# A head's second scores, one stretch of products sooner in the first two batches

## The chip, the cores and the metric

The kernel runs on one core of a Trainium2 chip. What counts is the device time of one execution in microseconds (us). TensorE (PE in the profile) multiplies matrices, VectorE (DVE), ScalarE (ACT) and GpSimd (POOL) work on tiles, SyncE (SP) issues transfers. Each has its own queue of instructions.

## The reference

An attention layer over 4 batches of 12 heads, 448 tokens and 64 numbers to a head, and behind it two layers of the feed-forward kind over all 1792 tokens:

```python
q_n, k_n = (rmsnorm(q, g_q), rmsnorm(k, g_k))
scores = scale * np.matmul(q_n, k_n.transpose(0, 1, 3, 2))
scores = scores - np.max(scores, axis=-1, keepdims=True)
attn = np.exp(scores)
attn = attn / (np.sum(attn, axis=-1, keepdims=True) + 1e-09)
x = np.matmul(attn, v)                      # then (1792, 768)
h = x @ w_in;  r = np.maximum(h, 0.0);  x = (r * r) @ w_out
a = x @ w1;  b = x @ w2;  out = ((a * b) @ w3) @ w_out2
```

The last two products have no function between them, so the kernel multiplies their weights (`w3` and the second `w_out`) once, ahead of the layers.

## The kernel before, in words

The 48 heads run one after the other in the loop `for h in range(NH + 1)`; H is 12, the heads of a batch. The attention of a batch leaves TensorE much time, and into that time the kernel puts dense products, which a generator hands out: in heads 0 to 12 those of `w3` with `w_out2` (384 products of 384 columns, tile `mm`), from head 13 on the feed-forward layers of the batch before (1008 products of 448 columns for a batch). Each call `fill(n)` hands out one stretch of them. A head has six stretches: about five products each up to head 12, and 12 or 15 each in heads 13 to 23 (the second batch, in which a pace is set layer by layer). After head 23 the same loop goes on with the third and fourth batch, and it ends with the layers of the last batch alone.

Every product is done in three passes, because a number is held as a high and a low half: `hl` is the tile of weights with both halves. The weights of the first round come from the inputs as 64-bit words. SP loads them (`raw<-w_in`, `raw<-w_out`, `raw<-w`), ScalarE and GpSimd work on the two words (L201, L207), VectorE joins them (L214), ScalarE copies the high half (`hl<-raw`, L113) and GpSimd or VectorE subtracts the low half (`hl<-raw,hl`, L121). SP also stores the joined weights for later batches. There are four buffers of 64-bit weights, six of joined ones and four of `hl`.

The parts of a head:

- `stage_k(h + 1)`: four transposes of the next head's keys (tile `kv`, L517) and a copy by ScalarE (`kt`).
- `stage_qk(h, s)`: the scores of half s, four products (L533, L534) into two buffers `sc` in PSUM, the only two there are. VectorE takes the maxima (`nb<-sc`, L535, twice) and scales them (`nb<-nb,rr`, L536).
- `stage_exp(h, s)`: ScalarE's two exponentials of the half (`p<-sc,nb,rr`, L552). Each frees one buffer `sc`. From head 12 on, SP then copies the half with a DMA (`pw<-p`, L558).
- `stage_t(h - 1, kc)`: four transposes each of the head before (tile `pt`, L579). They read both halves of `p` or `pw`. ScalarE copies the high half (`ptr`, `pte`), and `stage_lo` has VectorE subtract the low half.
- `stage_v(h - 1)`: seven products with the values (tile `kv`, L631).

So a head's first scores and its second scores take turns in the same two buffers, and both must wait until ScalarE has done the exponentials of the half before. Tile's scheduler orders each engine's queue by what it expects to be ready. Mostly it keeps the order of the code, but it may move an instruction past its neighbours. On the chip each queue then runs in that order.

Of the kernel before, what the change touches and what calls it, by code (L numbers as in the profile page):

```python
# [30 lines left out]
def attention_moe_kernel(  # L31
# [16 lines left out]
    B, P, H, C, D = q_nat.shape  # L48
# [62 lines left out]
    def copy_on(eng, out, in_):  # L111
        if eng == "a":
            nc.scalar.activation(out=out, in_=in_, func=AF.Copy)  # L113
        elif eng == "g":
            nc.gpsimd.tensor_scalar(out=out, in0=in_, scalar1=1.0, scalar2=1.0, op0=ALU.mult, op1=ALU.mult)
        else:
            nc.vector.tensor_copy(out=out, in_=in_)
# [280 lines left out]
    def load_group(g):  # L398
        if not (0 <= g < NH // GH):
            return  # L400
        b, h0 = divmod(g * GH, H)
        qn = t1.tile([P, GH, C, D], F32, name="qn", tag="qn")
        kn = t2.tile([P, GH, C, D], F32, name="kn", tag="kn")
        if g == 0:
            nc.sync.dma_start(out=kn[:, 0:1], in_=k_nat[0, :, 0:1])
            load_head(0)
            nc.sync.dma_start(out=qn[:, 0:1], in_=q_nat[0, :, 0:1])
            load_to(0)
            nc.sync.dma_start(out=kn[:, 1:], in_=k_nat[0, :, 1:GH])
            nc.sync.dma_start(out=qn[:, 1:], in_=q_nat[0, :, 1:GH])  # L410
            load_to(1)
        else:
            nc.sync.dma_start(out=kn, in_=k_nat[b, :, h0:h0 + GH])
            nc.sync.dma_start(out=qn, in_=q_nat[b, :, h0:h0 + GH])
        grp[g] = [qn, kn, None, None]

    def load_head(h):
        if not (0 <= h < NH):
            return
        b, hh = divmod(h, H)  # L420
        t = t2.tile([128, S], F32, name="qt", tag="qt")
        nc.sync.dma_start(out=t, in_=q_t[b, hh])
        qts[h] = t

    def load_v(h):
        if not (0 <= h < NH):
            return
        b, hh = divmod(h, H)
        t = t2.tile([128, C, D], F32, name="v", tag="v")
        nc.sync.dma_start(out=t, in_=v_in[b, hh])  # L430
        vs[h] = t
# [78 lines left out]
    def stage_k(h):  # L510
        if not (0 <= h < NH):
            return
        d = heads[h]
        khl = d.pop("khl")
        ps = ps_kv.tile([128, 512], F32R, name="kv", tag="kv")
        for c in range(C):
            nc.tensor.transpose(ps[:, c * P:(c + 1) * P], khl[:, c, :], ident_r)  # L517
        kt = t2.tile([128, S], F32R, name="kt", tag="kt")
        copy_on("a", kt, ps[:, :S].bitcast(F32))
        d["kt"] = kt  # L520

    def stage_qk(h, s):
        if not (0 <= h < NH):
            return
        d = heads[h]
        nb = d["nb"] = small.tile([P, 2], F32, name="nb", tag="nb")
        c0 = 2 * s
        o = d["sc"] = [None, None]
        for j in range(2):
            c = c0 + j  # L530
            ps = ps_sc.tile([128, 512], F32, name="sc", tag="sc")
            o[j] = ps[:P, :S]
            nc.tensor.matmul(o[j], d["qh"][:, c * P:(c + 1) * P], d["kt"], start=True, stop=False)  # L533
            nc.tensor.matmul(o[j], d["ql"][:, c * P:(c + 1) * P], d["kt"], start=False, stop=True)  # L534
            nc.vector.tensor_reduce(out=nb[:, j:j + 1], in_=o[j], axis=AX.X, op=ALU.max, negate=True)  # L535
        nc.vector.tensor_tensor(out=nb, in0=nb, in1=d["rq"][:, c0:c0 + 2], op=ALU.mult)  # L536

    def stage_exp(h, s):
        if not (0 <= h < NH):
            return  # L540
        d = heads[h]
        nb, o = d.pop("nb"), d.pop("sc")
        i = h % 2
        if s == 0 and i == 0:
            sums2[h // 2] = small.tile([P, 2, C], F32, name="sm", tag="sm")
        sm = sums2[h // 2]
        c0 = 2 * s
        pp = t3.tile([P, 2, S], F32, name="p", tag="p")
        for j in range(2):
            c = c0 + j  # L550
            p = d["p"][c] = pp[:, j, :]
            nc.scalar.activation(  # L552
                out=p, in_=o[j], func=AF.Exp, scale=d["rq"][:, c:c + 1], bias=nb[:, j:j + 1],
                accum_out=sm[:, i, c:c + 1],
            )
        if h >= H:
            words = t3.tile([P, 2, S], F32R, name="pw", tag="pw")
            nc.sync.dma_start(out=words.bitcast(F32), in_=pp)  # L558
            d["p"][c0:c0 + 2] = [words[:, 0, :], words[:, 1, :]]
        if s == 1 and i == 1:  # L560
            nc.vector.tensor_scalar(out=sm, in0=sm, scalar1=1e-9, scalar2=None, op0=ALU.add)
            rs = small.tile([P, 2, C], F32, name="rs", tag="rs")
            nc.vector.reciprocal(out=rs, in_=sm)
            wide = t1.tile([P, C, 2, D], F32, name="rsw", tag="rsw")
            nc.gpsimd.tensor_scalar(
                out=wide, in0=rs.rearrange("p i c -> p c i").unsqueeze(3).to_broadcast([P, C, 2, D]),
                scalar1=1.0, scalar2=1.0, op0=ALU.mult, op1=ALU.mult,
            )
            sums2[h // 2] = wide.rearrange("p c i d -> p c (i d)")
# [21 lines left out]
    def stage_lo(h):  # L591
        if not (0 <= h < NH):
            return
        d = heads[h]
        for lo, p, hi in d["lo"]:
            sub_on("v", lo, p, hi)
        d["lo"] = []
# [25 lines left out]
    def stage_v(h):  # L623
        if not (0 <= h < NH):
            return
        d = heads.pop(h)
        vt = d["v"].rearrange("p c a d -> p c (a d)")
        ps = ps_kv.tile([128, 512], F32, name="kv", tag="kv")
        ops = [(vt[:, kc, :], m) for kc in range(4) for m in d["pt"][kc]]
        for n, (w, m) in enumerate(ops):  # L630
            nc.tensor.matmul(ps[:, :S], w, m, start=(n == 0), stop=(n == len(ops) - 1))  # L631
        i = h % 2
        r0, r1 = i * D, (1 - i) * D
        if i == 0:
            xf[0] = t2.tile([128, S], F32, name="xf", tag="xf")
        x = xf[0]
        tmp = t1.tile([128, S], F32, name="vt", tag="vt")
        copy_on("a", tmp[r0:r0 + D, :], ps[r1:r1 + D, :S])
        nc.vector.tensor_tensor(out=x[r0:r0 + D, :], in0=ps[r0:r0 + D, :S], in1=tmp[r0:r0 + D, :], op=ALU.add)

    def stage_x(h):
        if 0 <= h < NH and h % 2:
            x = xf[0]
            b, hh = divmod(h, H)
            nc.vector.tensor_tensor(out=x, in0=norms_to_rows(h), in1=x, op=ALU.mult)
            t = xp.tile([128, 2, S], F32R, name="x", tag="x")
            copy_on("a", t[:, 0, :], x)
            sub_on("g", t[:, 1, :], x, t[:, 0, :].bitcast(F32))
            xs[b, hh // 2] = t
# [4 lines left out]
    def start_fill(gen, total):  # L654
        state.update(gen=gen, credit=0.0, left=total)

    def fill(n):
        state["credit"] += n
        while state["gen"] is not None and state["credit"] > 0:
            try:  # L660
                k = next(state["gen"])
                state["credit"] -= k
                state["left"] -= k
            except StopIteration:
                state["gen"] = None
# [22 lines left out]
    for h in range(NH + 1):  # L688
        n = W3O / ((H + 1) * 6) if h <= H else MOE / (H * 6)
        load_head(h + 3)  # L690
        load_v(h + 1)
        if h % GH == 0:
            load_group(h // GH + 1)
        stage_qk(h, 0)
        fill(n)
        stage_exp(h, 0)
        if h % H != 1:
            stage_x(h - 2)
        stage_t(h - 1, 0)
        stage_t(h - 1, 1)  # L700
        fill(n)
        stage_lo(h - 1)
        if h < NH:
            v_prep(h)
        fill(n)
        stage_k(h + 1)
        stage_t(h - 1, 2)
        stage_t(h - 1, 3)
        fill(n)
        stage_lo(h - 1)  # L710
        stage_qk(h, 1)
        fill(n)
        stage_exp(h, 1)
        fill(n)
        stage_v(h - 1)
        if h % GH == 1:
            group_prep(h // GH + 1)
        head_prep(h + 2)
        if h and h % H == 0:
            fill(1e9)  # L720
            stage_x(h - 1)
            start_fill(gen_moe(h // H - 1), MOE)
# [57 lines left out]
```

## Time and profile before

| | |
|---|---|
| median of 3 runs | 1230.52 us (1227.25 to 1230.81) |
| the profiled execution | 1229.23 us |
| its span, first to last instruction | 1227.4 us |
| TensorE busy | 1173.1 us, 96% |
| VectorE, ScalarE, GpSimd busy | 689.3, 732.9, 780.1 us |
| moved by DMA | 207.63 MB, mean 169 GB/s |

The span lies 1.8 us under the time of its own execution. Busy time is time in which the engine worked on an instruction, whatever kept it from working faster. What TensorE does not work adds up to 54.3 us.

### The profile page before, as it was taken

Reading aid. Unit: us, or ns where it says so; the run is one execution under the profiler, and the core shown is the slowest. Engines: PE = TensorE matmul, PEld = TensorE weight load, DVE = VectorE, ACT = ScalarE, POOL = GpSimd, SP = SyncE. Lnnn points to the kernel's source line nnn. Section 1 sums busy time; section 2 is a strip of 40 time slices with the busy share of each in tenths; the row PEclk is TensorE's granted clock in tenths of the full one; section 3 lists DMA queues with packets and bytes.
Section 4 is the critical chain, followed back from the end, with each engine's and each line's share of the span. In section 5 each row is a group of like instructions: output and inputs, shape, how many; then the busy total and the mean of one; then the engine's idle time right before and its main releaser. Section 6 shows DMA issues by size and latency. Waiting matters only on the chain.

```text
span 1227.4 us, 19009 instructions
## 1 busy us (share of the span) xinstructions
PE 1173.1 (96%) x6258; PEld 1054.9 (86%) x6258; DVE 689.3 (56%) x1231; ACT 732.9 (60%) x1581; POOL 780.1 (64%) x772
## 2 busy tenths in 40 slices
PE   7799999998989999999999999999999999999998
PEld 4588888886878889998998999999999999999998
DVE  5699878858977773556575554745655421012100
ACT  5799877767657564666646556656545544442442
POOL 6775535655666664766776664756766556678673
PEclk9699999999999999999999999999999999999999
DMA  7775447888788865545535455444543443333342
GB/s 230 228 252 163 148 143 231 276 280 268 253 264 260 252 193 167 147 132 149 161 113 169 133 174 159 145 128 136 156 121 114 139 138 116 111 111 103 103 129 72
DMA packets 111346, 207.63 MB, mean 169 GB/s; under 512 B 12208, under 2 KB 66704, under 8 KB 111248
## 3 DMA queue, kind: packets, MB, share of 16 engines
q1 hardware_dynamic: 107792, 200.92, 53.5%
q10 hardware_dynamic: 3456, 5.51, 1.2%
q8 instruction: 49, 0.80, 0.3%
q14 instruction: 49, 0.40, 0.1%
HBM read 149.95 MB, written 27.53 MB: 145 GB/s over the span
## 4 chain that ended last, share of the span: by engine, by line
PE 60%; DMA 4%; DVE 3%; POOL 2%; ACT 1%; issue 1%; SPq 0%; DVEq 0%; POOLq 0%; ACTq 0%
PE mm L269 17%; PE mm L271 17%; PE mm L270 17%; PE kv L631 3%; PE pt L579 2%; DMA raw<-w 2%; DMA pw<-p 2%; PE sc L534 1%; PE sc L533 1%; POOL hl L121 1%; DMA kn<-k_nat 1%; PE kv L517 1%; DVE raw L214 0%; POOL x L121 0%; PE mm L620 0%
## 5 line engine op out<-in xcount | busy, mean ns | idle before, releaser
L121 POOL TENSOR_TENSOR hl<-raw,hl 128x384 fp32r<-128x384 f32 (+1 forms) x383 | 446.5, 1169 | 259.6 <-ACT hl L113 253.5
L113 ACT ACTIVATE hl<-raw 128x384 fp32r<-128x384 f32 (+1 forms) x416 | 233.8, 564 | 147.7 <-PE mm L271 84.5
L270 PE MATMUL mm<-x,hl 128*128 128x448 f32 (+1 forms) x832 | 305.8, 368 | 7.6 <-POOL x L121 7.6
L269 PE MATMUL mm<-x,hl 128*128 128x448 f32 (+1 forms) x832 | 309.4, 372 | 1.6 <-DVE gf L342 1.0
L271 PE MATMUL mm<-x,hl 128*128 128x448 f32 (+1 forms) x832 | 305.0, 367 | 3.0 <-DVE hl L121 1.8
L270 PE MATMUL mm<-act,hl 128*128 128x448 f32 (+1 forms) x640 | 235.8, 368 | 4.3 <-POOL act L121 4.3
L269 PE MATMUL mm<-act,hl 128*128 128x448 f32 (+1 forms) x640 | 237.6, 371 | 0.0
L271 PE MATMUL mm<-act,hl 128*128 128x448 f32 (+1 forms) x640 | 234.4, 366 | 0.7 <-DVE hl L121 0.7
L552 ACT ACTIVATE p<-sc,nb,rr 112x448 f32<-112x448 f32 x192 | 137.3, 719 | 73.1 <-DVE nb L536 72.3
L270 PEld LDWEIGHTS mm<-x,hl 128*128 128x128 f32 x832 | 157.5, 189 | 21.5 <-POOL x L121 9.3
L271 PEld LDWEIGHTS mm<-x,hl 128*128 128x128 f32 x832 | 157.3, 189 | 17.9 <-POOL hl L121 3.1
L269 PEld LDWEIGHTS mm<-x,hl 128*128 128x128 f32 x832 | 157.3, 189 | 15.3 <-DVE gf L342 1.4
L270 PEld LDWEIGHTS mm<-act,hl 128*128 128x128 f32 x640 | 121.6, 190 | 16.2 <-POOL act L121 6.9
L535 DVE TENSOR_REDUCE nb<-sc 112x1 f32<-112x448 f32 x192 | 113.5, 617 | 36.8 <-PE sc L534 35.2
L271 PEld LDWEIGHTS mm<-act,hl 128*128 128x128 f32 x640 | 121.7, 190 | 10.6 <-DVE hl L121 1.1
L269 PEld LDWEIGHTS mm<-act,hl 128*128 128x128 f32 x640 | 121.6, 190 | 9.6
L121 DVE TENSOR_TENSOR ptr<-pt,ptr 128x448 fp32r<-128x448 f32 x144 | 86.8, 619 | 73.1 <-ACT ptr L113 72.6
L207 POOL TENSOR_SCALAR raw<-raw 128x384 uint32<-128x384 uint16 (+1 forms) x110 | 78.7, 716 | 66.1 <-DMA raw<-w_in 21.4
L214 DVE SCALAR_TENSOR_TENSOR raw<-raw 128x384 uint32<-128x384 uint32 (+1 forms) x120 | 80.9, 679 | 43.5 <-POOL hl L121 26.6
L121 POOL TENSOR_TENSOR act<-gf,act 128x448 fp32r<-128x448 f32 x80 | 97.8, 1223 | 8.9 <-DVE gf L342 3.7
L201 ACT ACTIVATE raw<-raw 128x384 f32<-128x384 f32 (+1 forms) x120 | 70.6, 598 | 52.6 <-DMA raw<-w_out 16.8
L342 DVE TENSOR_TENSOR gf<-mm,r 128x448 f32<-128x448 f32 x64 | 39.8, 622 | 94.7 <-ACT r L338 89.4
(87 smaller groups left out, 1595.2 us busy)
## 6 DMA issues: line engine op xcount, KB each, us to landing
pw<-p SPq DMA_DIRECT2D x72, 392.0 KB, 4.4
raw<-f_in SPq DMA_DIRECT2D x96, 192.0 KB, 2.4
raw<-f_out SPq DMA_DIRECT2D x72, 256.0 KB, 2.7
raw<-f SPq DMA_DIRECT2D x96, 192.0 KB, 2.3
raw<-w_in SPq DMA_DIRECT2D x32, 384.0 KB, 4.6
raw<-w_out SPq DMA_DIRECT2D x24, 512.0 KB, 5.9
raw<-w SPq DMA_DIRECT2D x32, 384.0 KB, 5.0
raw<-w3o SPq DMA_DIRECT2D x48, 256.0 KB, 2.7
```

What stands on the lines that cost most here:

```text
L113: nc.scalar.activation(out=out, in_=in_, func=AF.Copy)
L121: e.tensor_tensor(out=out, in0=in0, in1=in1, op=ALU.subtract)
L201: nc.scalar.activation(out=hi, in_=hi, func=AF.Prelu, scale=2.0**-112, alpha=-(2.0**32))
L207: nc.gpsimd.tensor_scalar(out=t[:, :n, 0], in0=low, scalar1=2.0**-13, scalar2=2.0**-14 - 0.5, op0=ALU.mult, op1=ALU.add)
L214: nc.vector.scalar_tensor_tensor(out=f[:, :n].bitcast(U32), in0=t[:, :n, 1], scalar=3, in1=t[:, :n, 0], op0=ALU.logical_shift_left, op1=AL ...
L269: nc.tensor.matmul(ps, w[:, 0, wk, :], x[0], start=(i == 0), stop=False)
L270: nc.tensor.matmul(ps, w[:, 0, wk, :], x[1], start=False, stop=False)
L271: nc.tensor.matmul(ps, w[:, 1, wk, :], x[0], start=False, stop=(i == last))
L342: nc.vector.tensor_tensor(out=gf, in0=ps, in1=r, op=ALU.mult)
L535: nc.vector.tensor_reduce(out=nb[:, j:j + 1], in_=o[j], axis=AX.X, op=ALU.max, negate=True)
L552: nc.scalar.activation(out=p, in_=o[j], func=AF.Exp, scale=d["rq"][:, c:c + 1], bias=nb[:, j:j + 1], accum_out=sm[:, i, c:c + 1],)
L631: nc.tensor.matmul(ps[:, :S], w, m, start=(n == 0), stop=(n == len(ops) - 1))
```

## The change

In heads 0 to 23 `stage_qk(h, 1)` is called ahead of `stage_k(h + 1)` and of the third and fourth group of transposes, and so one stretch of products sooner. The call of `fill` that stood behind it goes behind `stage_exp(h, 1)`. The number of stretches in a head stays six. Heads 24 to 47 keep their order.

```diff
         fill(n)
+        even = h < 2 * H
+        if even:
+            stage_qk(h, 1)
         stage_k(h + 1)
         stage_t(h - 1, 2)
         stage_t(h - 1, 3)
         fill(n)
         stage_lo(h - 1)
-        stage_qk(h, 1)
-        fill(n)
+        if not even:
+            stage_qk(h, 1)
+            fill(n)
         stage_exp(h, 1)
         fill(n)
+        if even:
+            fill(n)
         stage_v(h - 1)
```

On TensorE's queue in the second batch the four score products leave the place behind a stretch and stand ahead of the key transposes. This is where head 17's second scores come to stand:

```order
 L270 MATMUL mm<-x,hl 128x448
 L271 MATMUL mm<-x,hl 128x448
+L533 MATMUL sc<-kt,qh 112x448
+L534 MATMUL sc<-kt,ql 112x448
+L533 MATMUL sc<-kt,qh 112x448
+L534 MATMUL sc<-kt,ql 112x448
 L517 MATMUL kv<-ident_r,khl 128x112 x4
 L579 MATMUL pt<-ident_r,pw 128x112 x4
```

They move up past four key transposes, eight `pt` transposes and the 12 products (15 in other heads) of one stretch. So 36 to 45 products now lie between the second scores and the next head's first scores, where 24 to 33 lay before.

On ScalarE's queue the exponentials move too. The place is head 16's second half, before:

```order
L113 ACTIVATE kt<-kv 128x448
L113 ACTIVATE ptr<-pt 128x448
L113 ACTIVATE pte<-pt 64x448
L201 ACTIVATE raw_3474<-raw_3474 128x384
L113 ACTIVATE acc<-mm 128x448
L113 ACTIVATE hl<-raw 128x384
L201 ACTIVATE raw_3535<-raw_3535 128x384
L113 ACTIVATE hl<-raw 128x384
L201 ACTIVATE raw_3582<-raw_3582 128x384
L552 ACTIVATE p,sm<-sc,nb,rr 112x448 x2
```

and the same place now:

```order
L113 ACTIVATE kt<-kv 128x448
L113 ACTIVATE ptr<-pt 128x448
L113 ACTIVATE pte<-pt 64x448
L552 ACTIVATE p,sm<-sc,nb,rr 112x448 x2
L113 ACTIVATE acc<-mm 128x448
L113 ACTIVATE hl<-raw 128x384
L201 ACTIVATE raw_3474<-raw_3474 128x384
L201 ACTIVATE raw_3535<-raw_3535 128x384
L113 ACTIVATE hl<-raw 128x384
L201 ACTIVATE raw_3582<-raw_3582 128x384
```

The two exponentials of the second half pass six instructions, among them two copies of high halves of weights (`hl<-raw`) and three first steps on 64-bit words (`raw<-raw`), which now stand behind them.

In the first batch the scheduler keeps less of the code's order. This is head 10's second scores now, on TensorE's queue, where before they stood behind the transposes and six more products:

```order
L270 MATMUL mm<-act,hl 128x384
L271 MATMUL mm<-act,hl 128x384
L533 MATMUL sc<-kt,qh 112x448
L534 MATMUL sc<-kt,ql 112x448
L533 MATMUL sc<-kt,qh 112x448
L534 MATMUL sc<-kt,ql 112x448
L517 MATMUL kv<-ident_r,khl 128x112 x4
L579 MATMUL pt<-ident,p 128x112 x4
L269 MATMUL mm<-act,hl 128x384
L270 MATMUL mm<-act,hl 128x384
L579 MATMUL pt<-ident,p 64x112 x4
```

## Rows read from the trace of the kernel before

**Rows 1.** Busy time of each engine in four stretches of the span.

```profile
core 0: us, PE busy (x) PEld busy (x) DVE busy (x) ACT busy (x) POOL busy (x), PEclk, DMA share, GB/s
0.00:75.00 75.00, 56.65 (x259) 41.72 (x259) 51.89 (x94) 53.40 (x114) 53.90 (x64) 0.84 0.74 229
75.00:178.00 103.00, 96.29 (x591) 86.05 (x592) 88.44 (x174) 86.53 (x194) 53.65 (x68) 1.00 0.54 170
178.00:453.00 275.00, 250.63 (x1323) 221.34 (x1324) 221.78 (x394) 183.58 (x404) 168.74 (x182) 0.98 0.80 252
453.00:1227.00 774.00, 769.49 (x4088) 705.78 (x4087) 327.14 (x571) 409.40 (x872) 503.86 (x459) 1.00 0.45 134
```

**Rows 2.** TensorE's waits, 75 to 178 us: total us, times, longest us.

```profile
PE sc L533 <- ACT p L552: 5.5, 5, 1.8
```

**Rows 3.** TensorE's waits, 178 to 453 us.

```profile
PE sc L533 <- ACT p L552: 10.2, 10, 2.4
PE pt L579 <- DMA pw<-p: 7.3, 7, 1.8
PE mm L271 <- DVE hl L121: 2.6, 2, 1.8
```

**Rows 4.** TensorE in order of time, heads 16 to 17.

```profile
272.24 0.37 PE L533 MATMUL sc<-kt,qh 128*112 128x448 f32 x1
...
278.41 1.38 PE L631 MATMUL kv<-ptr,vhl 128*128 128x448 f32 x6
...
281.36 0.46 PE L533 MATMUL sc<-kt,qh 128*112 128x448 f32 x1 [1.38 <-ACT p L552]
...
297.22 0.37 PE L533 MATMUL sc<-kt,qh 128*112 128x448 f32 x1
```

**Rows 5.** VectorE in order of time, same heads.

```profile
278.08 0.56 DVE L214 SCALAR_TENSOR_TENSOR raw<-raw 128x384 uint32<-128x384 uint32 x1 [1.51 <-POOL hl L121]
278.56 1.15 DVE L535 TENSOR_REDUCE nb<-sc 112x1 f32<-112x448 f32 x2
...
279.98 0.48 DVE L536 TENSOR_TENSOR nb<-nb,rr 112x2 f32<-112x2 f32 x1
```

**Rows 6.** ScalarE in order of time, same heads.

```profile
280.50 0.72 ACT L552 ACTIVATE p<-sc,nb,rr 112x448 f32<-112x448 f32 x1 [0.56 <-DVE nb L536]
...
290.78 0.73 ACT L552 ACTIVATE p<-sc,nb,rr 112x448 f32<-112x448 f32 x1 [0.68 <-DVE nb L536]
```

**Rows 7.** TensorE in order of time, heads 10 to 11.

```profile
154.05 0.46 PE L533 MATMUL sc<-kt,qh 128*112 128x448 f32 x1 [1.25 <-ACT p L552]
...
157.68 0.46 PE L517 MATMUL kv<-ident_r,khl 112*128 112x112 f32 x4
...
159.84 0.36 PE L533 MATMUL sc<-kt,qh 128*112 128x448 f32 x1
...
164.15 0.46 PE L533 MATMUL sc<-kt,qh 128*112 128x448 f32 x1 [0.32 <-ACT p L552]
```

**Rows 8.** ScalarE in order of time, heads 10 to 11.

```profile
157.96 0.70 ACT L552 ACTIVATE p<-sc,nb,rr 112x448 f32<-112x448 f32 x1
...
163.28 0.72 ACT L552 ACTIVATE p<-sc,nb,rr 112x448 f32<-112x448 f32 x1 [0.79 <-DVE nb L536]
```

**Rows 9.** Two of three stretches of 3.4 us at the half clock.

```profile
305.70:309.10 3.40, 3.40 (x11) 2.91 (x10) 3.40 (x6) 3.40 (x9) 1.82 (x2) 0.51 0.49 170
...
411.60:415.00 3.40, 3.40 (x11) 3.01 (x10) 2.48 (x6) 1.77 (x4) 2.85 (x4) 0.50 0.95 270
```

**Rows 10.** ScalarE's waits, 178 to 453 us.

```profile
ACT p L552 <- DVE nb L536: 23.8, 14, 4.9
```

**Rows 11.** DMA issues of the page: KB each, median us to landing.

```profile
pw<-p SPq DMA_DIRECT2D x72, 392.0 KB, 4.4
```

**Rows 12.** The chain of waits, 178 to 440 us, a piece of it.

```profile
406.25 3.63 DMA raw<-w
...
411.82 5.64 DMA raw<-w
```

## The prediction

> **What bounds the kernel now.** I read the busy times by stretch first. From 453 us on TensorE works 769.5 of 774 us, and nothing but its own work sets the time there. What it loses lies ahead of that: 18 us up to 75 us, 6.7 us from 75 to 178 us and 24.4 us from 178 to 453 us [rows 1]. The last two stretches are the heads that the change touches, apart from the first three. A microsecond that TensorE stops losing there should arrive at the end whole, since behind 453 us nobody but TensorE is waited for.
>
> TensorE's list of waits says what it lost them to. From 75 to 178 us it is nearly all one wait, first or second scores for ScalarE's exponentials: 5.5 us in 5 times [rows 2]. From 178 to 453 us the same wait takes 10.2 us in 10 times, and 7.3 us in 7 times go to transposes that wait for the DMA of `pw` [rows 3].
>
> The order of time shows which scores wait. Head 16's second scores start at 272.24 us, head 17's first ones at 281.36 us after a wait of 1.38 us, and head 17's second scores start at 297.22 us without one [rows 4]. In between, VectorE takes the maxima of head 16's second half only at 278.56 us, 6.3 us after the scores began, because a join of weights stood in front that had waited 1.51 us for GpSimd [rows 5]. ScalarE then waits 0.56 us for `nb`, and its exponential at 280.50 us frees the first buffer at 281.22 [rows 6]. TensorE starts 0.14 us behind that. On the other side, head 17's first exponential frees its buffer at 290.78 + 0.73 = 291.51 us [rows 6], 5.7 us before the second scores want it. So one side waits and the other has room.
>
> **The change part by part.** No instruction is added or removed. What moves is the second scores, with the maxima, the exponentials and (second batch) the DMA of `pw` that follow from them.
>
> How far: between 272.24 and 278.41 us lie 4 scores and 24 products, so one such matmul takes 6.17 / 28 = 0.22 us [rows 4]. A stretch of 12 is 2.6 us. Four key transposes, eight `pt` transposes and six products of 384 columns take 159.84 - 157.68 = 2.2 us in head 10 [rows 7]. The six products are about 1.1 us by the same 0.22 us reduced to 384 of 448 columns, which leaves about 1.0 us for the twelve transposes. The second scores come 3.6 us sooner in the second batch and 2.2 us sooner in the first, where a stretch is five or six products.
>
> - First scores of the second batch. The exponential may now end 3.6 us later relative to the next first scores, and the longest wait is 2.4 us [rows 3]. All 10.2 us can go. The second scores spend 3.6 of their 5.7 us of room. Because the first scores lose their own wait, they start earlier against the same queue of VectorE, and the room shrinks by up to 1.4 us more. I charge 3 us for new waits there, between 0 and 10.2. Net: -7.
> - The DMA of `pw`. It lands 4.4 us after its issue [rows 11], and the longest wait for it is 1.8 us [rows 3]. The transposes of the next head come 3.6 us later after the second scores than before, and the exponentials pass six instructions on ScalarE's queue. I take 6.5 of 7.3 us. Bounds 0 and 7.3.
> - The clock. Three times in the second batch the granted clock stands at 0.50 to 0.51 for 3.4 us, 1.2 of 2.4 GHz; two of them are shown [rows 9]. 11 matmuls start in each, where 3.4 / 0.22 = 15 to 16 fit: 1.0 us lost by that count, 1.7 us by half the time. If TensorE idles less, fewer should come. I take two of three away at 1.3 us each: -2.6. Bounds 0 and -5.1.
> - What is given back in the second batch. These terms sum to 7 + 6.5 + 2.6 = 16 us. The chain of waits of this stretch runs through loads of weights, 3.63 us at 406 us and 5.64 us at 412 us [rows 12], VectorE works 222 of 275 us and the DMA engines 80% of the time [rows 1]. In 259 us in place of 275 they would have to be at 86% and 85%. TensorE already waits 2.6 us for low halves of weights [rows 3]; where these arrive just in time, time saved ahead of them is waited out there. I keep 6 tenths, 9.6 us, the middle of a loss of everything and none, somewhat to the good side because TensorE's waits for weights are a quarter of those for scores now.
> - The first batch. Head 10's first scores start at 154.05 us, its second ones 5.8 us later and head 11's first ones 4.3 us after these, with a wait of 0.32 us [rows 7]. The first exponentials free a buffer at 157.96 + 0.70 = 158.66 us, 4.6 us after the first scores, the second at 163.28 + 0.72 = 164.00 us, 4.2 us after the second [rows 8]. Moved by 2.2 us, the second scores would stand 3.6 us behind the first, one microsecond before their buffer is free; the next first scores would wait no more. The wait changes places, at about the size that it had. Of 5.5 us [rows 2] I take 2 as gained, between -6 (0.7 us lost in each of nine heads) and 5.5.
> - Up to 75 us no engine is busy for more than 57 us, and the DMA engines are at 74% [rows 1]: I read this stretch as one that waits for its first loads, which the change doesn't touch, and cost it at nothing.
>
> The sum: 1229.2 - 9.6 - 2 = 1217.6, say 1217 us. The profiled execution lies 1.3 us under the median of 1230.5, and 1.8 us over its span.
>
> **A rule that speaks against it.** The exponentials of the second half now stand right behind `pte` on ScalarE's queue, and everything behind them waits when `nb` is late. ScalarE already lost 23.8 us in 14 times to `nb` in the second batch, 4.9 us at most [rows 10]. The Trainium skill, "TensorE: Matmul & The Clock Gate", section "Architectural detail: the array is 16× 32×32, not 1× 128×128", says that ScalarE and VectorE are strict FIFO, which these waits agree with. Going by it alone, the copies of high halves behind the exponentials are late by each such wait, and the sum would turn to a loss (the fourth rival).
>
> **The rivals.**
> - Most waits go and part is given back (my forecast), 1210 to 1223 us: 0.50.
> - All of it is kept, and all three half clocks go: 1229.2 - 10.2 - 7.3 - 5.1 = 1206.6 us, and 4 of the first batch's 5.5 us as well: 1203 us. For it: TensorE hardly waits for weights now. Against: the chain through the loads [rows 12]. 0.16.
> - The weights pace the second batch. Waits for scores and `pw` become waits of the products for `hl`, and only the first batch's 2 us stay: 1227 us, 1222 to 1231. For it: the chain, and VectorE at 81%. Against: 17.5 us of waits that are not for weights. 0.20.
> - Slower: ScalarE stands in front of the second half's exponentials. In head 16 `nb` was ready at 279.98 + 0.48 us, 8.2 us after the second scores began [rows 4, 5]. By an estimate ScalarE is through `pte` 3.9 us after them: 0.8 us of scores, 1.0 us of transposes, three copies at no more than an exponential's 0.7 us each [rows 6]. It would then idle some 4 us in each of 11 heads, with two copies of weights waiting behind it. The point from which it decides is weights that are less than 4 us ahead of TensorE. With 2 us paid in each head that is 22 us, less the 13 us of waits that go: 1238 us. 0.09.
> - It changes nothing but the place of the wait: two buffers are too few wherever the scores stand, and 0.7 us more is lost in each of nine heads of the first batch: 1229.2 + 6 = 1235 us. 0.05. "Perfetto Trace Analysis" of the Trainium skill, section "Optimization Strategy", says that a gap repeating on the engine that should be saturated can mean too few buffers for the next tile. By that the move would give nothing in either batch. The 5.7 us of room on one side speak against it in the second batch, and the first batch's 4.6 and 4.2 us for it.
>
> **How the numbers follow.** A measurement of this kernel can't tell less than about 0.3%, 3.7 us, from no change: faster is below 1226.8 us. All of the first two cases and 0.08 of the third are faster: 0.74. Of the third 0.11, and 0.03 of the others, lie within: 0.14. The rest is slower: 0.12. The range reaches from the second case to just above the third, 1203 to 1232 us, which leaves out half of the second (0.08) and most of the slower ones (0.12).
>
> **What would show it.** TensorE's wait for exponentials from 178 to 453 us should fall from 10.2 us to about 3, with what is left in front of second scores, and the wait for `pw` to about 1. The second batch should end some 10 us sooner, and fewer than three half clocks should lie in it. The first batch should still show the wait, now at second scores. I am wrong if waits of products for `hl` grow by more than 6 us, if ScalarE's wait for `nb` grows well beyond 23.8 us, or if the stretch from 75 to 178 us becomes longer.

## The result, and the profile after

The changed kernel takes 1239.22 us (median of 4 runs, 1236.52 to 1240.40), the kernel before on the same chip 1230.26 us: ratio 1.0077, 95% interval 1.0059 to 1.0095. It is slower by 9 us. The prediction was wrong in sign, and its range ended 7 us below the result.

Where the 11 us of the profiled execution are lost (its span is 1238.5 us) is best read at fixed places of the program, not at fixed times. This table has the start of the last value product (`kv<-pte,vhl`, L631) of four heads, in us, from the order of time on TensorE. Head n stands for pass n of the loop, whose value products are those of the head before. Its last two columns belong to experiments below.

| head | before | after | change in heads 0 to 11 alone | in 12 to 23 alone |
|---|---|---|---|---|
| 1 | 75.62 | 76.60 | 76.77 | 76.17 |
| 7 | 138.95 | 144.56 | 144.01 | 140.03 |
| 12 | 209.26 | 214.92 | 215.06 | 208.26 |
| 23 | 488.31 | 499.68 | 497.39 | 491.75 |

So heads 2 to 7 lose 4.6 us, heads 8 to 12 nothing, and the second batch loses 5.7 us. Behind it nothing more is lost. The busy times of the kernel after, in the stretches of [rows 1]:

```profile
core 0: us, PE busy (x) PEld busy (x) DVE busy (x) ACT busy (x) POOL busy (x), PEclk, DMA share, GB/s
75.00:178.00 103.00, 94.60 (x574) 84.41 (x573) 89.67 (x169) 85.76 (x191) 53.77 (x68) 0.98 0.55 160
178.00:453.00 275.00, 247.03 (x1288) 217.15 (x1287) 231.26 (x387) 176.97 (x391) 169.03 (x177) 0.97 0.78 247
453.00:1239.00 786.00, 780.03 (x4145) 714.76 (x4143) 336.50 (x584) 416.44 (x888) 512.23 (x466) 1.00 0.45 135
```

TensorE starts fewer matmuls in both stretches (574 and 1288 where 591 and 1323 stood), and VectorE is 9.5 us busier in the second one. TensorE's waits of the kernel after, 178 to 453 us, which answer to [rows 3]:

```profile
PE mm L271 <- POOL hl L121: 7.2, 8, 2.2
PE mm L269 <- ACT hl L113: 5.7, 4, 2.5
PE mm L271 <- DVE hl L121: 4.1, 4, 1.7
PE sc L533 <- ACT p L552: 2.7, 1, 2.7
PE mm L270 <- DVE act L121: 2.4, 1, 2.4
PE mm L269 <- DVE gf L374: 2.0, 1, 2.0
PE pt L579 <- DMA pw<-p: 1.2, 1, 1.2
```

The waits that the change was costed by have gone as forecast: scores from 10.2 to 2.7 us, `pw` from 7.3 to 1.2 us. In their place stand 17.0 us in which products wait for the halves of weights (`hl`), of which the kernel before had 3.4 us, and 4.4 us for `act` and `gf` of the layers (2.5 us before). One such place, ScalarE in the kernel after:

```profile
314.24 0.52 ACT L113 ACTIVATE hl<-raw 128x384 fp32r<-128x384 f32 x1
314.78 0.55 ACT L113 ACTIVATE vt<-kv 64x448 f32<-64x448 f32 x1
321.33 0.66 ACT L201 ACTIVATE raw<-raw 128x512 f32<-128x512 f32 x1 [6.00 <-DMA raw<-w_out]
322.00 0.54 ACT L338 ACTIVATE r<-mm 128x448 f32<-128x448 f32 x1
322.45 0.51 ACT L113 ACTIVATE hl<-raw 128x384 fp32r<-128x384 f32 x1
```

and TensorE behind it:

```profile
323.01 0.47 PE L269 MATMUL mm<-x,hl 128*128 128x448 f32 x1 [1.81 <-ACT hl L113]
```

The high half that TensorE needs at once is the last row. In ScalarE's queue it stands behind the first step on another weight, one that is used later and whose load has not landed: ScalarE stands 6.00 us in front of a step that nobody needs yet. The kernel before has such waits too: from 178 to 453 us its ScalarE waits 44.1 us for loads of weights, and 50.3 us in the kernel after. What is new is that products wait behind them; before, none waited for a high half.

In heads 2 to 7 it is mostly the head's own low halves (`ptr`, `pte`) that come late. TensorE's waits of the kernel after from 76.7 to 144.7 us, complete; the same view of the kernel before, from 75.6 to 138.9 us, has one row, 1.4 us for scores:

```profile
PE kv L631 <- DVE ptr L121: 2.0, 2, 1.1
PE sc L533 <- ACT p L552: 1.7, 2, 1.3
PE kv L517 <- DVE xf L645: 0.9, 1, 0.9
PE kv L620 <- POOL raw L207: 0.8, 1, 0.8
PE pt L579 <- DVE ptr L121: 0.5, 1, 0.5
PE kv L631 <- DVE pte L121: 0.2, 1, 0.2
```

These are 6.1 us, 4.7 more than before, which is the 4.6 us of the table; 2.7 us of them are for `ptr` and `pte`. The longest wait for `ptr`, seen on VectorE, kernel after:

```profile
117.77 1.08 DVE L214 SCALAR_TENSOR_TENSOR raw<-raw 128x384 uint32<-128x384 uint32 x1 [1.76 <-POOL hl L121]
118.78 0.61 DVE L121 TENSOR_TENSOR ptr<-pt,ptr 128x448 fp32r<-128x448 f32 x1
119.42 0.62 DVE L121 TENSOR_TENSOR pte<-pt,pte 64x448 fp32r<-64x448 f32 x1
```

and on TensorE:

```profile
119.44 0.47 PE L631 MATMUL kv<-ptr,vhl 128*128 128x448 f32 x1 [1.06 <-DVE ptr L121]
```

The low half for the value product stands behind the join of a weight, and that join waited 1.76 us for GpSimd to finish with another weight's buffer. The other wait of 0.93 us for `ptr`, at 86.19 us, has no join in front: there the low half stands behind the scaling of the second scores' maxima (`nb`, 1.41 us), which in the kernel before comes after the head's low halves. So in the second batch, and in part in the first, work on weights stands in a queue in front of work that TensorE waits for.

### The profile page after: what moved, and what is told of

It is laid out like the page before. It is cut to its first block, busy times and chain, and to the rows that moved or that the text cites. A ratio compares the mean times of both kernels' runs of the same rounds, so it can differ in the third digit from the quotient of the medians.

```text
span 1238.5 us, 19031 instructions
## 1 busy us (share of the span) xinstructions
PE 1177.8 (95%) x6258; PEld 1056.6 (85%) x6258; DVE 709.5 (57%) x1231; ACT 731.8 (59%) x1581; POOL 786.3 (63%) x772
## 4 chain that ended last, share of the span: by engine, by line
PE 58%; DVE 2%; DMA 2%; POOL 1%; issue 1%; ACT 1%; DVEq 0%; POOLq 0%; SPq 0%
PE mm L269 17%; PE mm L271 16%; PE mm L270 16%; PE kv L631 3%; PE pt L579 2%; PE sc L534 1%; PE sc L533 1%; DMA pw<-p 1%; POOL hl L121 1%; PE kv L517 1%; PE mm L620 0%; DVE raw L214 0%; DMA kn<-k_nat 0%; DVE nb L535 0%; ACT p L552 0%
## 5 line engine op out<-in xcount | busy, mean ns | idle before, releaser
L269 PEld LDWEIGHTS mm<-act,hl 128*128 128x128 f32 x640 | 120.9, 189 | 11.8 <-ACT hl L113 0.8
L207 POOL TENSOR_SCALAR raw<-raw 128x384 uint32<-128x384 uint16 (+1 forms) x110 | 81.9, 744 | 66.4 <-DMA raw<-w_in 19.6
L214 DVE SCALAR_TENSOR_TENSOR raw<-raw 128x384 uint32<-128x384 uint32 (+1 forms) x120 | 94.0, 791 | 36.9 <-POOL hl L121 23.4
```

Source lines behind the costliest of these rows:

```text
L207: nc.gpsimd.tensor_scalar(out=t[:, :n, 0], in0=low, scalar1=2.0**-13, scalar2=2.0**-14 - 0.5, op0=ALU.mult, op1=ALU.add)
L214: nc.vector.scalar_tensor_tensor(out=f[:, :n].bitcast(U32), in0=t[:, :n, 1], scalar=3, in1=t[:, :n, 0], op0=ALU.logical_shift_left, op1=AL ...
L269: nc.tensor.matmul(ps, w[:, 0, wk, :], x[0], start=(i == 0), stop=False)
```

## The experiments

The theories were: the loss comes of the first round's weights, whose work stands in the same queues; or of the scores' own buffers, which would be too few in any place; or of SP, which stands at the issue of `pw` and holds up loads behind it. For the weights there were then three more: GpSimd's time, its second operand beside VectorE, and its wait for ScalarE's high half. "Moved" below means the change in heads 12 to 23 alone. All ratios are to the kernel before on the same chip; a line number is one to five lines higher where lines were added. A difference of one or two us between single traces is within what runs of one kernel differ by.

**Each batch alone.**

```diff
-        even = h < 2 * H
+        even = h < H          # the other run: H <= h < 2 * H
```

> The change in heads 0 to 11 alone. Theory A (two losses: in the first batch the second scores now come before their buffer is free, in the second batch the weights set the pace): about 6 us slower than before, all of it lost by the values' products of head 12, and TensorE's wait in front of second scores in the first batch stays at 7 to 10 us; the second batch loses no more. Theory B (the first batch loses and the second one only inherits it in another form): the whole 9 us. Theory C (the exponentials' place on ScalarE's queue in the second batch does the harm): about 0 to 2 us slower.

> The change in heads 12 to 23 alone. Theory A: 3 to 5 us slower, waits for scores and for the transfer of p nearly gone from 178 to 453 us, and products waiting for weights some 20 us in their place. Theory B: no difference to before, or faster by some us. Theory C: the 7 to 9 us that the first part does not explain.

Heads 0 to 11 alone: 1239.36 us, ratio 1.0076 (1.0051 to 1.0100). Heads 12 to 23 alone: 1234.83 us, 1.0040 (1.0026 to 1.0054). Each part loses by itself, and the whole change loses no more than the first part alone. Theory A foretold the second part rightly, and the first up to head 12. But with the change in the first batch alone the second, unchanged, loses another 3.3 us (the table), where theory A had nothing: its waits for `pw` from 195 to 465 us grew from 5.5 us to

```profile
PE pt L579 <- DMA pw<-p: 13.7, 9, 3.2
```

With the change in the second batch alone no wait for scores was left there, and the same stretch shows

```profile
PE mm L271 <- POOL hl L121: 11.9, 8, 2.2
PE mm L271 <- DVE hl L121: 4.6, 4, 2.7
PE mm L269 <- ACT hl L113: 2.9, 2, 2.2
```

**Without the weights' work.** The layers' weights are read, in all four rounds, from 32-bit tensors that exist already: no 64-bit loads, no steps on words, no joins, no stores for them. The weights of `w3` and `w_out2`, which are worked on up to about 110 us, keep theirs.

```diff
-            units.append((w64[i], w32[i]) if b == 0 else (w32[i], None))
+            n = w64.shape[-1]
+            units.append((q_t[i % B, i // B % H][:, :n] if n < 512 else w3o[i % (2 * NE)], None))
```

> The kernel before, in which the weights of all four rounds are read from other 32-bit tensors that are already there, so that no 64-bit weights of the layers are loaded, worked on as words, joined or stored: the output is not the reference's. This is the base for the next run. All theories: second batch shorter than in the kernel before, because the weights cost VectorE, ScalarE, GpSimd and the DMA engines much less; waits of first scores for exponentials should be left in part, some 3 to 8 us.

> The changed kernel with the same light weights (output not the reference's either). Theory A: with the weights out of the way the second batch gains what waits for scores and for the transfer of p were left in the run with light weights before, and loses nothing to weights; the first batch still loses about 6 us. Theory C (place of the exponentials on ScalarE's queue): the second batch stays as long as or longer than in the run with light weights before, with ScalarE waiting longer for nb.

Unchanged order: 1192.43 us, ratio 0.9686 (0.9657 to 0.9715). Changed order: 1192.60 us, 0.9690 (0.9663 to 0.9717). The loss is gone, and so is the gain. From 195 to 465 us the unchanged order has no wait for scores or `pw` left to win; its whole list is

```profile
PE mm L271 <- POOL x L121: 0.5, 1, 0.5
```

That is less than the 3 to 8 us that were expected. So both the waits that the prediction wanted to win back in the second batch and those that took their place come of the weights' work. Two buffers for scores are enough there without it. In the first batch they are not quite: scores still wait 5.5 us from 75 to 195 us in the old order and 3.5 us in the new one. There the new order comes to head 12 2.2 us sooner (206.41 against 208.61 us), where a loss of 6 us was expected. That gain lies in heads 8 to 12, which have no joins in this form. Heads 2 to 7, where seven joins are left after 75 us, gain nothing (0.7 us longer).

**Who issues `pw`.** ScalarE in place of SP, up to head 23, with the old order and with the moved one.

```diff
-            nc.sync.dma_start(out=words.bitcast(F32), in_=pp)
+            (nc.scalar if h < 2 * H else nc.sync).dma_start(out=words.bitcast(F32), in_=pp)
```

> The kernel before with the transfer of p into pw issued by ScalarE behind its exponentials, in place of SyncE, in heads 12 to 23. Base for the next run. Theory D (SyncE stands at the issue of pw until the exponentials are done, and the loads of weights behind it start late): SyncE's 35 us of waits for ScalarE at L558 go, and the kernel is 1 to 4 us faster than before. Theory E (VectorE's and GpSimd's work on the weights sets the pace): no difference beyond 0.3%, save for what the issue costs ScalarE.

> The change in heads 12 to 23 alone, with pw issued by ScalarE there. Theory D: SyncE's 68 us of waits for ScalarE at L558 go, products wait for weights at most as long as in the kernel before, and the 5 us that this half of the change loses turn into a gain. Theory E: still about 5 us slower than the run before it, with VectorE at some 226 of 270 us.

1244.00 us, ratio 1.0117 (1.0094 to 1.0141), and moved 1236.50 us, 1.0055 (1.0036 to 1.0074). Neither theory foretold this: the old order became 14 us slower, and on it the move wins 7.5 us. From 195 to 465 us the old order now has

```profile
PE pt L579 <- DMA pw<-p: 12.9, 9, 5.3
PE sc L533 <- ACT p L552: 8.4, 8, 2.4
```

and the move takes these 21.3 us down to 0.4. The waits of the moved kernel for `hl` stayed, 8.0 us for GpSimd's, 6.7 for ScalarE's, 4.7 for VectorE's; they are 7.6 us in the old order. So the move gives back 11.8 us in waits for weights, against 16.0 with SP issuing, and it gains because more was to win (20.9 us, against 12.6). SP's place at `pw` is not what makes weights late: its waits of 39.6 us at L558 in that stretch are gone, and its waits at the loads of weights (L187) for VectorE's joins rise from 62.8 to 129.9 us.

**GpSimd's low halves.** Four forms of this step in the first round, each with the old order and moved. First a copy of the joined weight, which needs no high half; then the copy done twice, so that GpSimd works at least as long as before; then a doubled copy of ScalarE's high half; then a difference of the joined weight and itself. All four leave out the true low half.

```diff
     def split_lo(i):
...
+        if U0 <= i < U1 and lo_eng[i % len(lo_eng)] == "g":
+            copy_on("g", t[:, 1, :n], raws.pop(i)[:, :n])
+            return
         sub_on(lo_eng[i % len(lo_eng)] if i < U1 else "g", t[:, 1, :n], raws.pop(i)[:, :n], t[:, 0, :n].bitcast(F32))
```

> The kernel before, in which GpSimd's low halves of the weights in the first round of the layers are a copy of the weights in place of a difference: GpSimd reads one tile where it read two (the output is not the reference's). Base for the next run. Theory E: VectorE's joins that lie beside it fall from 0.9 us on average to about 0.65, VectorE's busy time falls by 5 us or more, and the kernel gains some us. Theory D: no difference.

> The change in heads 12 to 23 alone, with the same copies by GpSimd. Theory E: joins beside GpSimd's work fall from 1.2 us on average to about 0.65, VectorE's busy time from 195 to 465 us falls from 226 us to 212 or less, and the loss against the run before it shrinks from 5 us to 0 to 2. Theory D: the loss stays at 5 us.

> The kernel before, with GpSimd's low halves of the first round's weights made as a copy of one tile, done twice, instead of a difference of two tiles (the low halves are wrong by that, and so the output). One copy took 0.63 and 0.78 us against 1.11 and 1.40 us of the difference, so that GpSimd is busy somewhat longer than in the kernel before, while it reads one tile at a time. If what the copy alone gave (12.6 us under before) came of GpSimd's time, this run gives it back: ratio 0.998 to 1.005, VectorE's joins as the others. If it came of what the two-tile differences do to VectorE's joins beside them, the gain stays: ratio near 0.990, and the joins of 512 columns stay near 0.75 us.

> The move in heads 12 to 23, with the same doubled copies on GpSimd. With single copies the move gained 7 us, with differences it lost 5 us. If the loss comes of GpSimd's time for the low halves: some 3 to 6 us above the unmoved kernel with doubled copies, and TensorE waits for low halves of GpSimd of some 10 us between 195 and 465 us. If it comes of GpSimd's differences lengthening VectorE's joins: still 4 to 8 us under it, and those waits under 4 us.

> The kernel before, with GpSimd's low halves of the first round made as a doubled copy of ScalarE's high half (the low halves are wrong by that, and so the output). So GpSimd waits for ScalarE's high halves as it did for the differences, is busy at least as long, and reads one tile at a time. No change in time is foretold by any theory for this one alone beyond 0.5% either way; it is the base for the moved one beside it.

> The move in heads 12 to 23 on that base. The copies of the raw weights let the move gain 6 to 7 us; they took away two things at once, the second tile that GpSimd reads beside VectorE and its wait for ScalarE's high half. If it is the two-tile reading that turns the gain into a loss: still 4 to 8 us under its base, joins on VectorE as in the base. If it is the wait for the high halves: 2 to 6 us over its base, with 8 us or more of waits of TensorE for GpSimd's low halves.

> The kernel before, with GpSimd's low halves of the first round made as a difference of the raw tile and itself (zeros, and so the output is not the reference's). GpSimd reads two operands beside VectorE, for as long as before, but needs not wait for ScalarE's high half. The base for the moved one beside it; within 1% of before by any theory.

> The move in heads 12 to 23 on that base. If the two-operand reading beside VectorE is the cause: 2 to 6 us over its base, VectorE's joins of 512 columns near 0.95 us against 0.75. If the wait for ScalarE's high halves is the cause: 4 to 8 us under its base, and the waits of TensorE for GpSimd's low halves under 3 us.

| GpSimd's low half | needs ScalarE's high half | old order | moved | moved less old | TensorE's waits for it, moved |
|---|---|---|---|---|---|
| the kernel's difference | yes | 1 | 1.0040 | +5 us | 11.9 us |
| copy of the weight | no | 0.9898 | 0.9848 | -6.9 us | none |
| the same twice | no | 0.9971 | 0.9925 | -6.3 us | 0.8 us |
| copy of the high half, twice | yes | 0.9918 | 0.9917 | -0.4 us | 8.6 us |
| weight less itself | no | 0.9971 | 0.9905 | -8.4 us | 0.7 us |

The intervals of the ratios are 0.0012 to 0.0028 wide to either side, so a difference of two of them is known to some 2 to 5 us. In the three forms that don't need the high half the move gains 6.3 to 8.4 us, where the prediction asked for 9.6. In the two that do it gains nothing. GpSimd's time isn't the cause: in the doubled copy it works 184.4 us from 195 to 465 us, in the moved kernel 173.0, and the gain stays, though that time costs either order some 9 us (0.9898 to 0.9971, 0.9848 to 0.9925). Nor is a second operand beside VectorE: the last form has one. In that form the three longest kinds of waits on TensorE, 195 to 465 us, are no longer for GpSimd's low halves (0.7 us are):

```profile
PE mm L273 <- DVE gf L346: 3.3, 1, 3.3
PE mm L273 <- ACT hl L113: 3.1, 2, 2.2
PE mm L275 <- DVE hl L121: 1.7, 1, 1.7
```

and in the form that needs the high half, on one operand, the two longest are:

```profile
PE mm L276 <- POOL hl L115: 8.6, 7, 2.8
PE mm L274 <- ACT hl L113: 2.2, 1, 2.2
```

Among these forms, what decides whether the move gains is the link from ScalarE's high half to GpSimd's low half. From 195 to 465 us the move makes TensorE's waits for all halves of weights grow by 16.0 us in the kernel itself and by 9.2 us in the form with the copy of the high half. Without the link they grow by 2.5, 7.5 and 5.3 us. What there is to win, waits for scores and `pw` in the old order, is not what sets these forms apart: 13.6 and 9.9 us with the link, 12.1, 16.2 and 13.5 us without.

Two things hang on that link and aren't separated. One is that the low half itself is late. The other is that GpSimd holds the joined weight's buffer longer: VectorE's waits for GpSimd at the joins are 23.8 us in the kernel before, and 7.3, 15.4, 0.9 and 9.7 us in the old order of the four forms. In the copy of the high half, which keeps the link but frees that buffer soonest, the move neither gains nor loses, against a forecast of 2 to 6 us of loss; so a late low half alone seems not to make the whole loss of 5 us. The scheduler also answers to the cut link. With the difference of the weight and itself, TensorE's order up to 560 us is that of the moved kernel, but many of GpSimd's low halves stand earlier in its queue. What the place in the queue does and what the wait does is not told apart.

**Fewer low halves for GpSimd**, with the computation whole: every second one on VectorE instead of every third.

```diff
-    LO_ENG = ("ggggv", "ggv")
+    LO_ENG = ("ggggv", "gv")
```

> The kernel before, with every second low half of the first round's weights on VectorE instead of every third. With the move this gave the time of before (1.0005), 4 us under the move alone. If the lighter GpSimd queue helps only where the move has made the weights late: 1.000 to 1.004. If it helps anyhow, and the move costs the same 5 us on it: 0.995 to 0.998.

> The move in heads 12 to 23, with every second low half of the first round's weights on VectorE instead of every third (the same values). GpSimd has then 24 differences of 144 fewer, VectorE as many more. If GpSimd's queue is what paces the weights: the waits for GpSimd's low halves go from 11.9 us to under 5, and the time falls under that of before, ratio 0.993 to 0.998. If VectorE is as full (226 us of the 270 there): the waits move to VectorE's low halves and joins, ratio 1.003 to 1.010.

Old order 1228.92 us, ratio 0.9995 (0.9978 to 1.0012), moved 1230.64 us, 1.0005 (0.9993 to 1.0017). Neither forecast came. The move's loss becomes too small to tell from nothing; 7.6 us of waits for GpSimd's low halves are left, and 4.8 for VectorE's. In the traces of the two, heads 13 to 23 still lose 5.4 us by the move (274.0 us to 279.4), and what balances it is won by head 12.

**Half as far.** The second scores go behind the transposes and ahead of the low halves' stretch, past one stretch of products alone: in the first batch, then in both.

```diff
         stage_t(h - 1, 3)
+        if even:
+            stage_qk(h, 1)
         fill(n)
         stage_lo(h - 1)
```

> The move in heads 0 to 11 alone, but only half as far: the second scores go behind the transposes and ahead of the low halves' stretch, some 1.1 us sooner instead of 2.2. The move of the whole stretch in these heads cost 9 us (ratio 1.0076). If the loss follows how far the scores are moved: 3 to 6 us, ratio 1.0025 to 1.005. If the loss begins only where the scores come to stand ahead of the exponentials' releases of the score buffers: within 2 us of before, ratio 0.998 to 1.002. If any other order of this stretch loses as much: ratio near 1.0075.

> The second scores half as far up (behind the transposes, ahead of the low halves' stretch) in heads 0 to 23. In heads 0 to 11 this gave 0.9988. If the second batch's loss comes only with the full move, as the first batch's did: 0.994 to 0.999. If any earlier place makes the weights late there: 1.001 to 1.005.

First batch: 1229.37 us, ratio 0.9988 (0.9978 to 0.9998). Both: 1235.27 us, 1.0034 (1.0018 to 1.0051). The first batch's loss is not in proportion to the distance. At half the way it is gone from the time of the whole. From 75 to 178 us TensorE's waits for scores fall from 5.5 to 0.3 us, and what it waits for instead is mostly

```profile
PE pt L579 <- DVE ptr L121: 3.5, 2, 2.2
```

In that trace heads 2 to 7 still lose 2.9 us, and heads 8 to 12 win 1.8 us back. In the second batch half the way loses as the whole way does. The kernel with both comes to head 12 at 207.67 us, ahead of the kernel before, and then loses 6.7 us up to head 23. No version here with the whole computation beats the kernel before by more than 0.12%.

## Why the prediction was wrong

**First scores and `pw` of the second batch** (-7 and -6.5): right. 10.2 and 7.3 us fell to 2.7 and 1.2, and the 2.7 stand at 188 us, still in the first batch.

**What is given back in the second batch**: this step failed. It kept 6 tenths of 16 us, because "TensorE's waits for weights are a quarter of those for scores now". All came back and 5.7 us more: waits of the products for `hl` rose from 3.4 to 17.0 us, where the prediction itself called a rise of 6 us the sign of being wrong. That these waits were few while TensorE stood waiting for scores said nothing of how many there would be without that. Without the weights' work neither wait exists, and with the link from high to low half cut the move gains 6 to 8 us. The runs put the lateness of the weights in the second batch at one link, ScalarE's high half to GpSimd's low half. The rival that the weights pace the second batch had this mechanism, but took it as a floor at which gain and loss cancel.

**A rule that speaks against it, and the fourth rival**: half right. The Trainium skill, "TensorE: Matmul & The Clock Gate", section "Architectural detail: the array is 16× 32×32, not 1× 128×128", calls the queues of ScalarE and VectorE strict FIFO, and the trace agrees: a high half stood behind a step that waited 6.00 us. But ScalarE did not stand at the exponentials, as that rival had it. Kernel after, ScalarE's waits from 178 to 453 us:

```profile
ACT raw L201 <- DMA raw<-w_out: 18.1, 7, 6.0
ACT p L552 <- DVE nb L536: 17.8, 13, 2.7
```

The wait for `nb` fell from 23.8 us [rows 10].

**The clock** (-2.6): wrong in sign. Three stretches of 3.4 us at the half clock [rows 9] became six times that length, two of them in the first batch, which had none. Kernel after, in windows:

```profile
162.40:165.81 3.41, 3.41 (x17) 3.01 (x18) 2.16 (x5) 2.17 (x5) 0.96 (x2) 0.51 0.38 134
189.71:193.12 3.41, 3.41 (x15) 3.36 (x14) 3.21 (x7) 2.91 (x7) 0.94 (x2) 0.51 0.83 238
285.29:292.11 6.82, 5.72 (x15) 4.52 (x16) 3.61 (x7) 3.99 (x10) 5.77 (x6) 0.51 0.93 261
```

Two more like them stand at 384.27 and 404.75 us. At the prediction's estimate of 1.0 to 1.7 us each, three more are 3 to 5 us. Yet heads 8 to 12, where the two of the first batch stand, lose nothing. In the second batch it is one more, 1 to 2 us. TensorE's waits between the table's rows of head 12 and head 23 sum to 25.6 us against 21.8. These 3.8 us and the clock's estimate together are about the 5.7 us lost there.

**The first batch** (-2, bounds -6 to 5.5): the size and the cause were wrong, the loss is 5.7 us up to head 12. The step weighed only the exponentials that free the score buffers. It did not look at VectorE and ScalarE, busy 58.2 and 59.0 of 64 us from 76 to 140 us already in the kernel before:

```profile
76.00:140.00 64.00, 62.10 (x384) 55.62 (x383) 58.15 (x118) 58.96 (x130) 37.62 (x48) 1.00 0.62 193
```

On VectorE the maxima, the low halves for the value product and the joins of weights share one queue, and 2.7 of the 4.7 us by which the waits grew in heads 2 to 7 are for such low halves. That this queue is the cause is read from the traces; no run changed it alone. That half the way costs nothing over the whole kernel says that room ends between the two places. The fifth rival, that two buffers are too few wherever the scores stand, named a loss of the right size. But without the work on the layers' weights the same two buffers cost the move at most 0.7 us in heads 2 to 7, and let it gain in heads 8 to 12. The Trainium skill, "Perfetto Trace Analysis", section "Optimization Strategy", says that repeating gaps can mean too few buffers for the next tile. If that were so here, the score waits from 178 to 453 us would have stayed; they fell by three quarters.

**Up to 75 us** (0): 1.0 us was lost there by head 1.

What stays open: why the unchanged second batch waits more for `pw` after a changed first one, how the lateness along the link divides between the low half and the held buffer, and what part of the first batch's loss is the weights'.

## What to carry to other kernels

A wait that is the longest on the engine that bounds the kernel may only be where another chain's lateness shows; take that chain's work out once, and see whether the wait itself goes and what the change is worth then, before costing the wait as gain. Where prefetch and the work at hand share in-order queues, look at what stands behind each instruction that waits for a load, and how far apart the links of one chain stand on two engines. A price list of moved waits has to include the queues of all engines that prepare work for the one that bounds the kernel, not only the one that releases the wait: VectorE was busy 91% of the first batch's stretch and 81% of the second's.

## What the runs showed of the hardware

VectorE's joins, the same instruction on the same shapes, changed their length with the order around them. From 195 to 465 us the 24 joins of 512 columns took 742 ns on average in the kernel before. In the moved kernel, and in the moved one where GpSimd takes the weight from itself, they are:

```profile
L214 DVE SCALAR_TENSOR_TENSOR raw<-raw 128x512 uint32<-128x512 uint32 x24 | 22.7, 957 | 3.2 <-POOL hl L121 1.5 <-POOL raw L207 1.2 <-issue 0.4
```

```profile
L214 DVE SCALAR_TENSOR_TENSOR raw<-raw 128x512 uint32<-128x512 uint32 x24 | 18.6, 786 | 4.6 <-POOL raw L207 4.0 <-issue 0.4 <-ACT raw L201 0.2
```

The Trainium skill, "SBUF — State Buffer", section "🔬 SBUF: two separate sides", says that a VectorE instruction with two inputs in SBUF and a GpSimd one that reads SBUF share a pair of ports, which the one that starts first holds for its whole length. The traces agree. In the moved kernel's stretch the five joins of 512 columns that no GpSimd instruction overlaps took 674 to 693 ns each. The twelve that overlap one with two inputs took 677 to 1785 ns, 1198 on average. Doubled copies on one operand lengthened joins too (832 to 861 ns on average). The lengthening did not decide the move: it gained with joins of 832 ns in one form and of 768 in another.
